# One two-bank PSUM tile for attention, then two one-bank tiles for layer 1 and Sinkhorn, with a new hand-written start order

## The chip, the core and the metric

The kernel runs on one core of one Trainium2 chip. The metric is device time in microseconds (us), the median of several executions. The profile is that of one further execution of the same program.

## What is computed

Linear attention over 8 batches, 8 heads, 576 positions and 64 channels feeds a mixture of 8 experts on 4608 tokens of width 512. The routing weights come from 8 Sinkhorn rounds over a 4608 x 8 matrix.

```python
phi = lambda x: np.where(x > 0, x, np.exp(x) - 1.0) + 1.0
q_p, k_p = phi(q), phi(k)
kv  = einsum('bhsd,bhse->bhde', k_p, v);   z = k_p.sum(axis=2)
x   = einsum('bhsd,bhde->bhse', q_p, kv) / (einsum('bhsd,bhd->bhs', q_p, z) + 1e-6)   # as [4608, 512]
logits = x @ w_gate;  P = exp(logits - logits.max())
for _ in range(8):
    P /= P.sum(1, keepdims=True) + 1e-9
    P /= P.sum(0, keepdims=True) + 1e-9
    P *= N / E
out = sum over e of  P[:, e:e+1] * (np.maximum(x @ w1[e], 0) @ w2[e])
```

## The kernel before

The kernel is a list of tasks for a small planner (`_Plan`). Each task has an engine (TensorE "pe", ScalarE "act", VectorE "dve", GpSimd's DMA issue "pool", SyncE's "sp", the transfer itself "dma", or "none" for bookkeeping), a planned duration, its predecessors and the buffers that it takes. The planner emits the tasks in the order of its planned start times. Each engine then executes its own instructions strictly in that order. The first 1465 tasks do not follow the planner's choice: their order is written out by hand in `_FRONT` (number of the task, letter of the engine). All waits between engines are put in by the tile framework: an instruction waits for the earlier instructions that wrote or read the same tile.

The stages are these.

- **Warm-up.** TensorE runs 46 dummy matmuls of 512 columns (line 575). They fill the time until attention's first inputs are there, and stand between attention's first steps after that.
- **Attention.** There are 16 groups (batch b, half g of the heads), n = 2b + g. A group loads k, q and v through one queue of GpSimd (line 366; the very first k goes through SyncE). ScalarE takes the exponentials of k and q (lines 376 and 435), VectorE builds phi (lines 380, 384, 438, 442). TensorE multiplies k and v ("KV", line 401), transposes q ("QT", line 427), multiplies for the denominator twice ("DEN", `f_den`, line 458) and for the numerator twice ("NUM", `f_num`, line 458). ScalarE inverts the denominator by Ln and Exp (lines 471, 476), and VectorE writes x, transposed, to `xT` (line 486). QT and DEN write the tile `at2`, 128 x 2 x 512 float32, two PSUM banks. KV and NUM share the other two-bank tile `kv_ps`.
- **Expert 0 as filler.** TensorE fills the gaps with layer 1 (line 659) and layer 2 (line 887) of expert 0 for the blocks of 512 tokens that attention has finished. The weights w1 of expert 0 come in four pieces and w2 in two, in the same GpSimd queue as q, k and v.
- **Logits and Sinkhorn.** Four small products (line 502) write a part of one bank of `at2`. When all are there, eight rounds run on VectorE (lines 526 to 536, 545 to 550), and in each a matmul with a matrix of ones sums over the partitions (line 541, `f_c`). It writes 8 columns of one bank of `at2`.
- **Experts 1 to 7.** From token block 5 of expert 0 on, layer 1 and layer 2 run as seven products of half size each (a Strassen-like scheme). `block7` is layer 1: two pairs per block, each with seven products of four matmuls (line 781), `m1` to `m7`. A pair holds three PSUM banks: `gX` (tile `hq`), `gZ` (tile `Zye`) and `gR`, which is one bank of `at2`, given out in turn by `att_bank()`. Into `gR` go `m5` (opens the bank) and `m3` (adds to it). Between them ScalarE copies it out (`f_s5`, line 807), and after them VectorE reads it once more (`f_h12`, line 816). Layer 2 is line 1005; VectorE adds its results to `acc` (line 1019), and builds the sums `S` (line 978), `W` (line 945) and `T` (line 957).

The order of the products from expert 1 on is a fixed chain on TensorE (lines 1089 to 1102).

PSUM has eight banks: two for `ye`, two for `hq`, two for `at2` and two for attention's `kv_ps`; the last two become `Zye` when attention is over (`f_close`).

```python
at2 = aps.tile([P, 2, 512], FP32, tag="att", name="att")           # line 256
def att_bank():                                                    # line 345
    return at2[:, (len(p_att["order"]) - 1) % 2]
```

Of the kernel before, what the change touches and what calls it, by code (L numbers as in the profile page):

```python
# [10 lines left out]
FP32 = mybir.dt.float32  # L11
# [6 lines left out]
class _Plan:  # L18
# [121 lines left out]
    1n 108n 119n 599n 109g 110m 48s 49m 2p 3p 50g 51m 4p 0g 5p 6p 52g 53m 7p 8p 76g 77m 9p 78g 79m 10p 11p 80g 81m  # L140
    12p 13p 14p 15p 126g 127m 16p 54a 55d 17p 18p 128g 129m 19p 20p 21p 22p 130g 131m 23p 24p 25p 26p 27p 61n 111g
    112m 62a 63d 28p 29p 56d 30p 31p 32p 33p 64d 34p 35p 36p 37p 57n 156g 157m 58p 65p 59a 82a 114g 115m 38p 66d 39p
    40p 83d 60a 89n 116g 117m 67p 84d 41p 68a 42p 91d 90a 69p 85n 154g 155m 43p 86p 70a 92d 158g 159m 71a 87d 93p
    133d 88a 94d 139n 182g 183m 132a 74p 95p 75d 44p 45p 96a 46p 134d 184g 185m 72p 140a 97p 73d 135n 47p 141d 98a
    136p 113n 186g 187m 142d 99a 137d 143p 138d 120g 121m 167n 600p 168a 144d 100p 101d 145p 601p 123g 124m 146a 169d
    102p 602p 103d 147p 603p 170d 148a 118n 210g 211m 604p 606p 149a 605d 608p 610p 161d 212g 213m 160a 152p 171p
    153d 612p 172a 162d 214g 215m 607d 163n 613a 164p 609d 611a 240g 241m 614p 165a 166d 189d 173p 195n 188a 242g
    243m 616p 615a 197d 190d 174a 150p 618p 268g 269m 196a 151d 191n 175p 636n 192p 176a 198d 177a 619d 199p 193d
    104g 105m 122n 622p 200d 194a 617a 180p 201p 181d 620p 202a 178p 203p 125n 179d 244g 245m 621p 204a 623p 628d
    106g 107m 217d 637p 639p 223n 216a 218d 270g 271m 224a 624p 225d 205a 226d 219n 272g 273m 220p 640d 638a 227p  # L150
    221a 298g 299m 641p 222a 228d 630a 208p 229p 253n 246a 302g 303m 209d 626p 230a 247d 643p 254a 642d 354g 355m
    231p 248d 206p 300g 301m 645p 232a 255d 207d 233a 625p 249n 256d 236p 644a 238p 237d 274a 281n 275d 250p 239a
    646a 257p 251d 330g 331m 647p 252d 258a 326g 327m 276d 649p 328g 329m 283d 282a 305d 259p 234p 627p 648a 235d
    277n 260a 651p 284d 650d 285p 669n 278p 286d 311n 304a 634a 261p 279d 358g 359m 670p 262a 280d 356g 357m 313d
    264p 263a 652d 287p 655p 671d 288a 265d 656p 312a 306d 266p 672p 267d 339n 307n 340a 289p 314d 308p 663a 290a
    659p 309d 386g 387m 332a 310d 384g 385m 315p 673d 292p 291a 382g 383m 316d 674p 341d 317p 632a 333d 660p 414g
    415m 318a 293d 676p 675a 342d 657p 361d 677a 360a 367n 334d 294p 319p 658p 295d 335n 320a 412g 413m 362d 336p
    321a 369d 343p 337d 416g 417m 678p 338a 344d 395n 440g 441m 665a 368a 324p 389d 345p 653p 325d 346a 679d 654p
    388a 322p 680p 323d 363n 396a 347p 397d 370d 364p 348a 661d 371p 446a 500g 501m 681d 682p 442g 443m 419d 365a
    686p 366a 372d 349a 352p 398d 296p 683a 390d 684p 297a 353d 667a 373p 685d 702n 350p 505g 374a 703p 496g 497m  # L160
    554n 560n 391n 351d 418a 425n 399p 392p 400d 468g 469m 375p 393d 444g 445m 688p 376a 394d 470g 471m 704d 689p
    377a 420d 401p 427d 378p 402a 687p 379d 696a 403p 447d 426a 380p 705p 381d 421n 404a 707p 448d 498g 499m 706d
    555g 556m 453n 474a 422p 428d 557g 558m 405a 692p 472g 473m 423a 429p 424a 709p 454a 430d 481n 408p 455d 710a
    431p 409d 693p 708a 578d 432a 406p 711p 407d 449n 694a 433p 456d 450p 434a 712d 435a 475d 457p 713p 476d 510n
    482a 483d 715p 458d 559n 451a 690p 452a 484d 714a 436p 700a 459p 437d 717p 460a 716d 438p 718a 461p 439d 477n
    691p 462a 512d 463a 503d 478p 735n 579d 485p 502a 479d 721p 486d 480a 736p 585d 504d 487p 722p 488a 580d 581s
    582m 466p 489p 467d 738p 490a 737d 511a 464p 410p 465d 506n 739a 698d 507p 411a 513d 740p 508a 729a 509a 514p
    741d 491a 742p 515d 492p 586d 516p 493d 719p 517a 564d 494p 518p 720p 565d 519a 566d 743d 725p 567s 568m 727a
    587d 520a 495d 726p 588s 589m 569s 570m 523p 723p 524d 583s 584m 744p 521p 746p 522d 724p 552n 747a 768d 745a
    772d 525p 733a 773d 748p 769d 774d 750p 731d 775s 776m 590s 591m 749d 754p 751a 779n 770d 526a 553p 527d 777s  # L170
    778m 755p 752p 780p 592d 528p 753p 781a 771d 794p 529d 782p 824d 786p 783a 762d 784p 787a 593d 788p 825d 796p
    571d 790p 797a 758p 760d 785a 791d 756p 795a 826d 530d 827s 828m 759p 792p 800p 757p 801a 766a 789d 798p 831n
    793a 804p 799a 531p 832p 805d 802p 833a 532d 806p 803d 838p 807a 764d 836p 839a 810p 594d 876d 595s 596m 834p
    597s 598m 533d 846p 835a 812p 837a 813p 847a 848p 877d 840p 849a 878d 842p 572d 854p 841d 852p 843d 811p 853a
    820a 855d 844p 818a 534p 850p 573d 845a 535d 814p 574s 575m 851a 536d 829s 830m 815p 856p 985s 986m 884p 576s
    577m 808p 885a 977d 809p 822d 857d 537p 886p 883n 538d 890p 887a 539d 866p 816a 891a 892p 888p 858p 889a 867p
    859a 893d 894p 874d 540p 898p 895d 864p 899a 541d 542d 896p 862p 897a 900p 902p 901a 863p 903a 928d 904p 929d
    865p 1042s 1043m 561g 562m 905a 930d 879s 880m 870a 881s 882m 906p 872d 543p 908p 544d 936p 909d 931s 932m 860p
    933s 934m 907d 861p 545d 938p 868a 935n 918p 937a 939a 919p 978d 910p 926a 546p 979d 942p 940p 547d 943a 944p
    911a 916p 945d 941a 563n 548d 946p 917p 950p 924a 952p 951a 914p 953a 947d 956p 980d 915p 957a 960p 954p 961d  # L180
    549p 948p 550d 962p 949a 551d 912p 922d 635a 958p 913p 631a 959d 1498n 1499g 1500m 963a 988p 1501g 1502m 920d
    987n 955a 970p 761d 989a 990p 976n 981d 763a 968p 982d 991a 994p 871d 996p 983d 995a 992p 697a 998p 971p 993a
    999d 699a 629d 969p 997d 1000p 975d 974a 1002p 1004p 1003a 964p 1005a 1503n 1008p 1010p 1009a 1006p 701a 1011d
    965p 1001a 984d 1012p 1007a 1045p 1013d 966p 1046a 633d 967p 1047p 973d 1044n 1504n 1014p 1048a 972d 1051p 1099s
    1100m 1015a 1053p 666a 1049p 1016d 1020p 1052a 1017d 1022p 1018d 1021a 662a 1019d 1025p 1050a 1023d 1055p 1024d
    664a 1030p 1056d 668d 1033p 1031d 1032d 1057p 1059p 1058a 1061p 1060a 1036p 1062a 1026a 1065p 1038d 1067p 1027g
    1037d 1066a 1063p 1054d 730a 1069p 1102p 1064a 1070d 1104p 1103a 1035d 1039p 1105a 1068d 1071p 1034d 1101n 1108p
    1040d 1072a 1156s 1157m 1041d 1110p 1109a 1073d 1106p 1028a 1077p 1074d 1029g 732d 1079p 1078a 1075d 734a 1082p
    1076d 1107a 1080d 1112p 1085a 1081d 1087p 873a 1113d 1086g 817a 869d 1090p 1089d 1083a 1088d 1114p 1084g 1111d
    1116p 1118p 728d 1117a 1093p 695d 1119a 927d 1115a 1092d 1122p 1091d 1124p 1123a 1095d 1120p 1094d 1126p 1121a  # L190
    1159p 1127d 1161p 1160a 1096p 1162a 1128p 1098d 1158n 1165p 1097d 1129a 1213s 1214m 1167p 1125d 1163p 1130d 1134p
    1131d 1136p 1135a 1132d 1166a 1139p 921d 1164a 1138d 1169p 1133d 1140a 1144p 1142a 1137d 1170d 1143g 1147p 1145d
    1141g 1146d 1171p 1148d 1173p 1172a 1508d 1175p 1174a 1150p 1509d 1176a 1168d 765a 1179p 1151d 1181p 1180a 1152d
    1177p 1183p 1178a 1216p 1184d 1218p 1217a 1149d 1153p 1219a 767d 1182d 1185p 1215n 1222p 1155d 1186a 1270s 1271m
    1154d 1224p 875a 823d 1220p 1187d 1191p 1223a 1188d 1193p 1192a 1189d 1196p 1190d 1195d 1226p 1199a 1194d 1201p
    1197a 1200g 1225d 1221a 1204p 1227d 1198g 1203d 1228p 1202d 1230p 1205d 1232p 1231a 1207p 1233a 1229a 1236p 1209d
    1238p 1206d 1237a 1234p 1239d 1240p 1235a 1273p 1208d 1275p 1241d 1274a 1210p 1276a 1242p 1212d 1272n 1279p 1211d
# [15 lines left out]
def kernel(  # L213
# [17 lines left out]
    P = 128  # L231
# [280 lines left out]
    def sinkhorn():  # L512
# [10 lines left out]
        for it in range(8):  # L523
# [15 lines left out]
            def f_c(_, gc=gc):  # L539
                gc["tile"] = att_bank()[:, 2 * E:3 * E]  # L540
                nc.tensor.matmul(gc["tile"], lhsT=ones_t, rhs=gs, start=True, stop=True)
# [65 lines left out]
    for b2, t in lg_pe.items():  # L607
        if 4 * b2 + 7 < len(kv_id):
            S_.dep(kv_id[4 * b2 + 7], t)
    p_done = sinkhorn()  # L610

    accp = []
    Zt = [None, None]

    def f_close(_):
# [521 lines left out]
```

## Time and profile before

| | |
|---|---|
| time, median of 3 runs | 970.51 us (969.93 to 971.1) |
| the profiled execution: its own time | 968.34 us |
| its span, first to last instruction | 966.5 us |
| granted TensorE clock over the span | 1.00 |
| TensorE matmul busy | 954.4 us (99% of the span), 8480 matmuls |
| VectorE busy | 774.7 us (80%) |
| ScalarE busy | 571.8 us (59%) |
| GpSimd busy | 145.8 us (15%) |

A row of the page's groups gives line, engine, operation, output<-inputs and shape, then the busy time of the group and the mean of one, then the idle time of the engine just before such instructions and what ended it. In a timeline, a row has its start, its length (merged rows are a run of equal instructions) and in brackets the idle time before it with the instruction that ended it. A matmul's row is longer than the distance between two matmuls, since the next one starts while the last one drains. So the idle time in brackets is less than what TensorE lost there.

### The profile page before, as it was taken

How to read it: one execution, taken by the hardware profiler on the slowest of the kernel's cores; microseconds unless marked ns; L12 is line 12 of the kernel's file. 1: busy time of each engine (PE TensorE's matmuls, PEld its weight loads, DVE VectorE, ACT ScalarE, POOL GpSimd, SP SyncE). 2: the span in 40 equal slices, each digit the busy share in tenths (PEclk: the TensorE clock that was granted, in tenths of full speed). 3: DMA queues.
4: the chain of work that ended last, by engine and by line, in shares of the span. 5: the costliest groups of instructions: out<-in, count | busy, mean ns of one | idle time of the engine just before them, and what ended most of it. 6: DMA issues, size and time to landing. Idle time of an engine off the chain costs nothing.

```text
span 966.5 us, 20909 instructions
## 1 busy us (share of the span) xinstructions
PE 954.4 (99%) x8480; PEld 795.6 (82%) x8480; DVE 774.7 (80%) x1484; ACT 571.8 (59%) x1017; POOL 145.8 (15%) x209
## 2 busy tenths in 40 slices
PE   8999999999999999999999999999999999999998
PEld 4565566688888888888888888888888888888886
DVE  5898898788878888878887888878887888877775
ACT  5898744665555555555555555555555555555553
POOL 6434000011022111111112111111112111111110
PEclk9999999999999999999999999999999999999999
DMA  9998646222257222262226322272225322235554
GB/s 224 260 203 187 158 143 207 45 77 78 77 120 163 79 77 78 86 156 77 78 76 123 113 70 73 74 159 71 76 77 132 107 77 77 78 99 164 164 164 109
DMA packets 45680, 112.50 MB, mean 116 GB/s; under 512 B 4368, under 2 KB 25616, under 8 KB 45584
## 3 DMA queue, kind: packets, MB, share of 16 engines
q1 hardware_dynamic: 21056, 75.57, 23.9%
q0 software_dynamic: 24128, 35.07, 19.3%
q8 instruction: 66, 1.08, 0.4%
q10 hardware_dynamic: 400, 0.52, 0.2%
q14 instruction: 30, 0.25, 0.1%
HBM read 119.69 MB, written 17.69 MB: 142 GB/s over the span
## 4 chain that ended last, share of the span: by engine, by line
PE 92%; DVE 3%; ACT 2%; issue 1%; DMA 1%; POOL 0%; DVEq 0%; POOLq 0%; ACTq 0%
PE ye L1005 32%; PE hq L781 23%; PE att L781 12%; PE ye L887 6%; PE Zye L781 6%; PE Zye L1005 5%; PE hq L659 3%; PE yw L575 1%; DVE h L816 1%; DVE acc L1019 1%; PE kv_ps L401 1%; PE att L458 1%; DVE S L978 1%; DMA kin<-in_k_dram 1%; PE num_ps L458 1%
## 5 line engine op out<-in xcount | busy, mean ns | idle before, releaser
L1019 DVE SCALAR_TENSOR_TENSOR acc<-ye,P_sb,acc 128x256 f32<-128x256 f32 x620 | 267.8, 479 | 123.9 <-PE ye L1005 122.9
L781 PEld LDWEIGHTS <-W 128*128 128x128 f16 x2144 | 209.8, 98 | 30.8 <-issue 2.5
L1005 PEld LDWEIGHTS <-S 128*128 128x128 f16 x1984 | 194.0, 98 | 23.4 <-DVE S L978 0.7
L1005 PE MATMUL ye<-T,S 128*128 128x256 f16 x1488 | 192.8, 273 | 0.4 <-DVE S L978 0.4
L1029 POOL TENSOR_TENSOR acc<-acc,st 128x256 f32<-128x256 f32 x124 | 88.1, 729 | 635.7 <-ACT st L1026 635.6
L781 PEld LDWEIGHTS <-w 128*128 128x128 f16 x1608 | 157.3, 98 | 21.2 <-issue 1.0
L813 ACT ACTIVATE h<-hq 128x512 f16<-128x512 f32 x134 | 80.0, 597 | 141.8 <-PE hq L781 140.6
L1005 PEld LDWEIGHTS <-h 128*128 128x128 f16 x1488 | 145.5, 98 | 17.6 <-issue 0.7
L781 PE MATMUL att<-xs,W 128*128 128x256 f16 x1008 | 151.2, 273 | 1.3 <-DVE h L816 1.2
L781 PE MATMUL hq<-xs,W 128*128 128x256 f16 x1008 | 151.2, 273 | 0.0
L781 PE MATMUL hq<-xs,w 128*128 128x256 f16 x1008 | 140.9, 273 | 0.3 <-DVE h L816 0.3
L810 ACT ACTIVATE h<-Zye 128x512 f16<-128x512 f32 x134 | 80.0, 597 | 38.3 <-PE Zye L781 38.3
L816 DVE CUSTOM_DVE_ANT_0 h<-att,s 128x512 f16<-128x512 f32 x126 | 86.5, 687 | 15.1 <-ACT s L800 13.0
L1026 ACT ACTIVATE st<-Zye,P_sb 128x256 f32<-128x256 f32 x124 | 52.7, 471 | 73.3 <-PE Zye L1005 73.3
L793 ACT COPY Zye<-hq 128x512 f32<-128x512 f32 x134 | 77.7, 580 | 28.9 <-PE hq L781 28.6
L978 DVE TENSOR_TENSOR S<-h 128x1024 f16<-128x1024 f16 x124 | 85.8, 692 | 11.0 <-ACT h L813 10.7
L800 ACT COPY s<-hq 128x512 f32<-128x512 f32 x126 | 73.5, 583 | 34.9 <-PE hq L781 34.8
L816 DVE CUSTOM_DVE_ANT_0 h<-hq,s 128x512 f16<-128x512 f32 x126 | 86.6, 687 | 4.0 <-PE hq L781 3.9
L887 PE MATMUL ye<-w,h 128*128 128x512 f16 x312 | 76.7, 379 | 0.0
L807 ACT COPY s<-att 128x512 f32<-128x512 f32 x126 | 74.6, 592 | 2.7 <-PE att L781 2.0
L781 PE MATMUL Zye<-xs,w 128*128 128x256 f16 x504 | 75.6, 273 | 0.0
L1005 PE MATMUL ye<-T,h 128*128 128x256 f16 x496 | 64.3, 273 | 0.3 <-DVE acc L1019 0.3
(104 smaller groups left out, 957.4 us busy)
## 6 DMA issues: line engine op xcount, KB each, us to landing
xs<-xd SPq DMA_DIRECT2D x63, 896.0 KB, 4.6
kin<-in_k_dram POOLq DMA_DIRECT2D x15, 576.0 KB, 6.9
out_dram<-acc SPq DMA_DIRECT2D x67, 128.0 KB, 2.4
w<-in_moe_w_dram POOLq DMA_DIRECT2D x16, 512.0 KB, 8.6
w<-in_moe_w_dram POOLq DMA_DIRECT2D x7, 1024.0 KB, 13.2
qin<-in_q_dram POOLq DMA_DIRECT2D x16, 288.0 KB, 6.2
vv<-in_v_dram POOLq DMA_DIRECT2D x16, 288.0 KB, 7.8
xd<-acc SPq DMA_DIRECT2D x5, 512.0 KB, 2.7
```

The source lines that it names most:

```text
L781: nc.tensor.matmul(dst[:, p, :], lhsT=lhs(p, c), rhs=rhs(c), start=(first and p == 0 and c == 0), stop=(c == 1), skip_group_check=True)
L793: nc.scalar.copy(out=Zt[1], in_=gX["tile"])
L800: nc.scalar.copy(out=gs2["tile"], in_=gX["tile"])
L807: nc.scalar.copy(out=gs5["tile"], in_=gR["tile"])
L810: nc.scalar.activation(out=hd(0, 0), in_=Zt[1], func=AF.Relu)
L813: nc.scalar.activation(out=hd(1, 0), in_=gX["tile"], func=AF.Relu)
L816: nc.vector._custom_dve(TENSOR_ADD_SAT, out=dst, in0=ps, in1=sb, s0=3.0e38, s1=0.0)
L887: nc.tensor.matmul(gy[tt]["tile"], lhsT=gh["tile"][:, f, ds(P * tt, P)], rhs=gw2["tile"][:, f, :], start=(f == 0), stop=(f == NFT - 1))
L978: nc.vector.tensor_tensor(out=Sx[:, i], in0=a0, in1=a1, op=op)
L1005: nc.tensor.matmul(bank(g_)[:, s, :], lhsT=lhs(s, kk), rhs=rhs(kk), start=(new and s == 0 and kk == 0), stop=(kk == 3), skip_group_check=True)
L1019: nc.vector.scalar_tensor_tensor(out=dst(), in0=bank(g_)[:, s, :], scalar=P_sb[:, gg, e:e + 1], in1=dst(), op0=ALU.mult, op1=ALU.add)
L1029: nc.gpsimd.tensor_tensor(out=dst(), in0=dst(), in1=gst["tile"], op=ALU.add)
```

## The change

There are three parts.

- **The tile.** The pool of `at2` gets a scope of its own (`aps_x`) and is placed at the other end of PSUM (`side="right"`). A new bookkeeping task `t_apsx`, after all of attention and all logits, closes it and opens in its place a pool with two tiles of one bank each, R0 and R1. `r_bank()` gives them out in the same turns as `att_bank()` did. Layer 1's `gR` and Sinkhorn's column sums use these; QT, DEN and the logits stay on `at2`. The first product into `gR` and the column sums get `t_apsx` as a further predecessor.
- **The planner's costs.** The transfer of a w1 piece goes from 1.6 to 1.4, the other weights from 2.75 to 2.6, and the latency of q, k and v from 2.3 to 2.2. These numbers only order the tasks behind the hand-written list.
- **The hand-written order.** `_FRONT` is replaced as a whole. Numbers from 527 on move by one, as `t_apsx` takes number 527. Task for task TensorE, GpSimd and SyncE have the same work in both lists, in another order. Of the tasks that may run on ScalarE or VectorE, some change sides; three of attention's copies of QT's result (`f_qc`, line 448) go from VectorE to ScalarE.

```diff
 _FRONT = """
-    1n 108n 119n 599n 109g 110m 48s 49m 2p 3p 50g 51m 4p 0g 5p 6p 52g 53m 7p 8p 76g 77m 9p 78g 79m 10p 11p 80g 81m
-    12p 13p 14p 15p 126g 127m 16p 54a 55d 17p 18p 128g 129m 19p 20p 21p 22p 130g 131m 23p 24p 25p 26p 27p 61n 111g
...
+    1n 104g 105m 108n 119n 600n 48s 49m 2p 3p 50g 51m 4p 76g 77m 5p 6p 52g 53m 7p 8p 78g 79m 9p 10p 126g 127m 54a 55d
+    11p 12p 80g 81m 13p 14p 15p 128g 129m 16p 56d 17p 18p 19p 130g 131m 20p 21p 22p 0g 23p 24p 25p 109g 110m 26p 27p
+    28p 82a 83d 29p 111g 112m 30p 31p 32p 33p 84d 34p 35p 36p 37p 38p 57n 58p 89n 61n 62a 63d 64d 156g 157m 65p 59a
...
 """
-    aps = ctx.enter_context(tc.tile_pool(name="aps", bufs=1, space=PSUM))
+    aps_x = ExitStack()
+    aps = aps_x.enter_context(tc.tile_pool(name="aps", bufs=1, space=PSUM, side="right"))
...
-                ts_.append(add(("dma", (1.6 if nm == "w1" and len(pieces) > 1 else 2.75)), lambda _: None, deps=[ti],
+                ts_.append(add(("dma", (1.4 if nm == "w1" and len(pieces) > 1 else 2.6)), lambda _: None, deps=[ti],
...
-            tin[nm] = fadd(("dma", 1.47 if nm == "k" else 1.42 if n else 2.3), lambda _: None, deps=[ti], use=[gr, *gsw], prio=pr, lat=2.3)
+            tin[nm] = fadd(("dma", 1.47 if nm == "k" else 1.42 if n else 2.3), lambda _: None, deps=[ti], use=[gr, *gsw], prio=pr, lat=2.2)
...
             def f_c(_, gc=gc):
-                gc["tile"] = att_bank()[:, 2 * E:3 * E]
+                gc["tile"] = r_bank()[:, 0, 2 * E:3 * E]
                 nc.tensor.matmul(gc["tile"], lhsT=ones_t, rhs=gs, start=True, stop=True)
...
-            c = add(("pe", 0.112), f_c, deps=[a], acq=[gc], prio=-200.0, lat=0.1)
+            c = add(("pe", 0.112), f_c, deps=[a, t_apsx], acq=[gc], prio=-200.0, lat=0.1)
...
+    Rt = []
+
+    def f_apsx(_):
+        aps_x.close()
+        rps = ctx.enter_context(tc.tile_pool(name="rps", bufs=1, space=PSUM, side="right"))
+        Rt.extend(rps.tile([P, 2, 256], FP32, tag=f"att{i}", name=f"R{i}") for i in range(2))
+
+    def r_bank():
+        return Rt[(len(p_att["order"]) - 1) % 2]
+    t_apsx = add(("none", 0.0), f_apsx, deps=[*front_ids, *lg_done], prio=0.0)
     p_done = sinkhorn()
...
                         g_["tile"] = (hqp.tile([P, 2, 256], FP32, tag="hq", name="hq") if g_ is gX else
-                                      att_bank().rearrange("p (a b) -> p a b", a=2))
+                                      r_bank())
...
-            m5 = pm(W(1, gi), T(1), gR, True, [m1, tW], 0.05)
+            m5 = pm(W(1, gi), T(1), gR, True, [m1, tW, t_apsx], 0.05)
```

In the list, 104 and 106 are the two tiny loads of the gate's weights, 109, 111, 114 and 116 the four pieces of expert 0's w1, 0 the identity matrix for QT; 48 to 53 are group 0's k, q and v, 76 to 81 group 1's, 126 to 131 group 2's. 54 and 82 are the exponentials of k of groups 0 and 1, 62 that of q of group 0; 2 to 47 are the dummy matmuls, 58 is KV and 65 QT of group 0.

## The prediction

> **What bounds the kernel now.** I read the page first.
>
> ```profile
> PE 954.4 (99%) x8480; PEld 795.6 (82%) x8480; DVE 774.7 (80%) x1484; ACT 571.8 (59%) x1017; POOL 145.8 (15%) x209
> PE   8999999999999999999999999999999999999998
> PEclk9999999999999999999999999999999999999999
> PE 92%; DVE 3%; ACT 2%; issue 1%; DMA 1%; POOL 0%; DVEq 0%; POOLq 0%; ACTq 0%
> ```
>
> TensorE is busy in 99% of the span at full granted clock, and holds 92% of the chain that ended last. Only the time in which it does no useful matmul can be won. The windows show where that is (columns: length, then busy us of each engine).
>
> ```profile
> 0.00:20.00 20.00, 16.43 (x105) 7.84 (x106) 9.86 (x19) 10.09 (x12) 13.87 (x25) 1.00 1.00 214
> 20.00:40.00 20.00, 18.77 (x156) 10.54 (x155) 17.68 (x29) 18.13 (x24) 8.85 (x12) 1.00 1.17 259
> 140.00:160.00 20.00, 19.58 (x132) 12.62 (x130) 18.04 (x44) 9.51 (x19) 0.00 (x0) 1.00 0.57 169
> 200.00:300.00 100.00, 97.97 (x885) 86.14 (x883) 82.77 (x162) 59.64 (x113) 13.97 (x19) 1.00 0.29 86
> 300.00:500.00 200.00, 200.00 (x1835) 179.26 (x1832) 160.42 (x309) 113.15 (x213) 27.14 (x38) 1.00 0.34 95
> 900.00:966.50 66.50, 62.30 (x546) 53.10 (x543) 45.33 (x88) 31.11 (x58) 6.55 (x10) 1.00 0.54 142
> ```
>
> Busy time flatters the start (dummy matmuls) and hides small waits (a matmul's row is longer than the distance to the next). So I made a ledger from the starts of all matmuls: each useful one counts its usual distance to the next (216 ns for 512 columns, 109 for 256 from line 781 on, 122 for line 458, 56 for QT, 45 for KV, 26 for logits), and the rest is lost. Lost by 24 us: 18.2; by 110: 22.4; by 140: 22.4; by 160: 23.5; by 200: 23.2; by 290: 27.0; by 945: 28.1; by 961: 28.7; after the last matmul 3.9 more. From 300 us on nothing is left to win but the tail, which keeps its instructions. What the change can touch: the start (18.2), attention (4.2, of which about 3.2 are the changes into and out of KV's half-height shape, 96 and 130 ns in each of 14 groups, and stay), 140 to 160 (1.1), 200 to 290 (3.8).
>
> Third, the group of products into the split tile, and a place in the timeline.
>
> ```profile
> L781 PE MATMUL att<-xs,W 128*128 128x256 f16 x1008 | 151.2, 273 | 1.3 <-DVE h L816 1.2
> ```
>
> ```profile
> 212.84 1.04 PE L781 MATMUL hq<-xs,w 128*128 128x256 f16 x8
> ...
> 213.62 0.67 DVE L816 CUSTOM_DVE_ANT_0 h<-att,s 128x512 f16<-128x512 f32 x1
> ...
> 214.34 0.60 PE L781 MATMUL att<-xs,W 128*128 128x256 f16 x4 [0.47 <-DVE h L816]
> ```
>
> Here m5 opens a bank of `at2` and waits until VectorE has read the pair before, which lies in the other bank. By the starts 0.63 us is lost. The waits written into the program of before confirm it: products into one half wait for readers of the other half. Following these waits through the trace gives seven stalls on VectorE's reading of the other bank: column sums at 148.17 us (0.17) and 157.82 (0.16), layer 1 at 214.34 (0.63), 229.29 (0.39), 255.82 (0.33), 283.74 (0.46) and 636.22 (0.09). Sum 2.24 us. Other waits into `att` in that time (131.45, 145.49, 266.55; 0.09, 0.40, 0.26) are on ScalarE's copy of the same bank and stay.
>
> **The two tiles.** They take away the seven waits. Upper end: all 2.24, plus every other wait of TensorE on VectorE or ScalarE from 140 to 290 us (2.5 more: 145.49, 147.57, 207.86, 211.97, 222.30, 266.55, 267.53, 281.54), if the new order loses none. Lower end: 0, if VectorE is late anyhow and TensorE meets it one product later. From 222 to 229 us VectorE was busy 6.84 of 7.00 us, so the 0.39 at 229.29 is its own lateness, and I count it as coming back. At the other six VectorE has slack nearby (5.75 of 8.00 us from 214 to 222, 13.19 of 17.00 from 267 to 284). I take 2.24 - 0.39 = 1.85 us won.
>
> The Trainium skill's page "PSUM — Partial Sum Buffer", section "PSUM bank collisions raise a hardware error", states that two engines collide by bank and quadrant, and run clean on different banks. By it alone all seven waits are needless and this term is 2.24, the time 0.39 us less than mine; the trace shows the waits, not what stands behind them.
>
> Closing and reopening issues no instruction. The first writers of R0 and R1 must wait for the old tile's last reader, the last logits' Exp, over at 126.0 us; the first column sum came at 128.5 and the first m5 at 130.1, so 2.5 us cover it. Without cover it would be the lateness of that Exp, for the column sum and the layer-1 products queued behind it. Another position in PSUM changes no row: 0. The planner's costs issue nothing.
>
> **The new order, start.** Landings are read from the trace's DMA records. In before, one w1 piece (256 KB) is ahead of q in GpSimd's queue; it landed at 6.88, then q0 8.42, v0 9.83, k1 11.29, q1 12.61, v1 14.12, k2 15.55, q2 16.88, v2 18.40, w1's second piece 19.66: one each 1.3 to 1.5 us. After, a 4 KB load (0.16 us by the pair at 45.72 and 45.88) goes first, both w1 pieces come behind v2, and k1 ahead of v0. q0 is issued at about 2.3. The shortest landing of such a load in the trace is 4.03 us, so it lands between 6.3 and 8.4; I take 7.0, one piece earlier. Then k1 8.5, v0 9.9, q1 11.3, k2 12.8, v1 14.2, q2 15.5, v2 17.0, the w1 pair 19.5. From group 4 on the same items have gone through, so the landings are the same.
>
> Now the three queues with before's durations (before's start in brackets). KV0 stands behind 37 dummies instead of 36, 0.21 each: 12.1 (11.89); QT0 12.95 (12.74). ScalarE does k1's Exp at 8.5 and q0's by 10.8, not at 13.18 between the two copies of KV0's result, so these end at 13.8 (14.73). DEN0 now waits for VectorE's copy of QT0: 14.5 (14.79). ScalarE then runs q1's Exp, Ln (14.95), k2's Exp, Ln to 17.45: KV1 16.0 (16.59), QT1 17.5 (17.88), NUM0 18.05 and 19.75 (19.30, 20.62), x of group 0 done 20.95 (21.90). KV2 21.0 (21.96), QT2 22.1 (23.19), NUM1 22.85 (24.14), DEN2 23.55 (24.79). Layer 1 starts at 23.8 (23.70), with NUM1 and DEN2 already behind it. QT3 26.65 (28.78), KV3 28.95 (30.54). In before four more layer-1 matmuls (4 x 0.216 = 0.87) come ahead of KV3: won 30.54 - 0.87 - 28.95 = 0.72 us. Ends: 1.5 if q1, k2 and the rest land early too; 0.9 lost if k1 lands at 11.29 as before, because q0's Exp is now queued behind k1's on ScalarE: Exp to 13.6, QT0 14.4, some 1.6 late.
>
> **The new order, attention.** The 14 shape changes stay. True waits after 24 us came to about 1 us. ScalarE gets three more copies (1.12 us each, VectorE's are 0.76): counted by rows, ScalarE's work up to the last Exp of attention rises from 94.4 to 96.4 us, VectorE's from 85.2 to 85.9. The trace shows no run of this order: between -0.8 and +5, by the rival below. I take 0, since the work per queue is the same within 2%.
>
> **Later order.** From the third product after the last column sum TensorE's sequence is nearly that of before and from expert 2 on the planner makes it by the same rule; 645 us there lost 1 us. 0.
>
> **Sum.** 0.72 + 1.85 = 2.57 us won. The profiled execution took 968.34 (span 966.5 and 1.8 around it), 2.17 below the runs' median of 970.51. So the next profile should show a span near 964.0 and its own time near 965.8, and the median 967.9 us. A difference under 0.2% (1.94 us) is about what can't be told from none.
>
> **Rivals.**
>
> - *Attention's queue is late* (slower). TensorE is in order and each of 16 groups puts seven products in its queue. In before about ten of these waited, 0.2 to 0.5 us each, 0.3 on average (for instance 30.54: 0.39, 58.82: 0.27, 80.94: 0.50). One more such wait per group costs 16 x 0.3 = 4.9 us, net 970.5 - 2.6 + 4.9 = 972.8. It decides from (1.94 + 2.57) / 16 = 0.28 us per group. For it: ScalarE was busy 18.1 to 18.5 of 20 us there and gets more; the whole list is new. Against: before's list, of the same kind, has few waits. 0.16.
> - *The wait moves* (same). VectorE is the late one from 200 to 290 us, the products wait one step later, or the two tiles still hold each other up, as they share a pool: only the start is won, 969.8. For it: 82.8% busy there with full stretches. Against: slack at six of seven places. 0.23.
> - *The start fails* (same): k1 late, 970.5 - 1.85 + 0.9 = 969.6. 0.07.
> - *More is won*: the new order has none of the other waits from 140 to 290 either: 970.5 - 0.7 - 2.2 - 2.0 = 965.6. 0.14.
> - *The forecast*, 967.2 to 968.6: 0.40.
>
> So faster by over 0.2%: 0.40 + 0.14 = 0.54; within 0.2%: 0.23 + 0.07 = 0.30; slower: 0.16. The range reaches from 965.0, just past the fourth rival, to 972.8, the middle of the first, which leaves half of 0.16 and a few hundredths out.
>
> **What would show it.** Right: the group `att` of line 781 without idle time on line 816; the windows 200 to 300 and 140 to 160 with TensorE nearer to full; KV3 near 29 us with four fewer layer-1 matmuls ahead. Wrong: q0 landing at 8.4 or k1 at 11.3; new idle rows at lines 401, 427 and 458 between 24 and 110 us, or a ledger there above 4.2; idle on VectorE's `acc` or `S` (lines 1019, 978) in place of line 816.

## The result and the profile after

The changed kernel takes 966.60 us (median of 6 runs, 965.53 to 968.68) against 970.23 us in the same comparison (6 runs, 969.56 to 971.42): ratio 0.9964, 95% interval 0.9950 to 0.9978. The forecast was 967.9. The profiled execution took 966.83 us, span 965.0. First its page:

```profile
PE 953.1 (99%) x8480; PEld 796.4 (83%) x8480; DVE 771.6 (80%) x1479; ACT 576.2 (60%) x1022; POOL 145.5 (15%) x209
PE   8999899999999999999999999999999999999998
PEclk9999999999999999999999999999999999999999
PE 93%; DMA 3%; DVE 2%; ACT 1%; issue 0%; POOL 0%; POOLq 0%; ACTq 0%; DVEq 0%
```

In the second row one slice, the fifth (97 to 121 us), has fallen to 8, and DMA has 3% of the chain instead of 1%. The windows (columns as before) say more:

```profile
110.00:120.00 10.00, 7.52 (x53) 3.98 (x51) 6.57 (x13) 6.04 (x8) 0.00 (x0) 0.83 0.79 187
140.00:160.00 20.00, 20.00 (x142) 13.68 (x140) 14.79 (x38) 11.50 (x22) 0.00 (x0) 1.00 0.64 206
200.00:300.00 100.00, 100.00 (x918) 89.57 (x916) 86.23 (x170) 59.92 (x113) 16.40 (x23) 1.00 0.37 100
```

From 140 to 160 and from 200 to 300 us TensorE is now busy without a gap (19.58 and 97.97 before). But from 110 to 120 us it is busy only 7.52 of 10 us, at a granted clock of 0.83: a stall that before did not have. The group of layer 1's products into the split tile has no idle time left (1.3 us before):

```profile
L792 PE MATMUL R<-xs,W 128*128 128x256 f16 x1008 | 151.2, 273 | 0.0
```

The ledger of the prediction, taken for every profile of this study, gives the us lost in four stretches. (A little below zero means that the usual distances were put a few ns too high; the small added matmuls of the last experiments count as lost time.)

| kernel | 0-24 | 24-110 | 110-130 | 130-300 | median us | ratio to before (interval) |
|---|---|---|---|---|---|---|
| before | 18.2 | 4.2 | 0.0 | 4.7 | 970.2 to 971.0 | |
| changed | 17.4 | 4.3 | 4.4 | -0.4 | 966.60 | 0.9964 (0.9950-0.9978) |
| changed, again | 17.4 | 3.9 | 3.9 | -0.4 | 965.96 | 0.9957 (0.9942-0.9973) |
| tiles only | 18.4 | 5.3 | 0.1 | 3.7 | 966.30 | 0.9953 (0.9936-0.9971) |
| order only | 17.7 | 5.9 | 2.8 | 5.1 | 971.86 | 1.0012 (1.0000-1.0024) |
| changed, loads early | 17.4 | 6.1 | 0.2 | -0.5 | 964.92 | 0.9941 (0.9928-0.9953) |
| the same, w1 piece first | 18.7 | 5.3 | 0.2 | -0.4 | 964.86 | 0.9934 (0.9922-0.9946) |
| order only, loads early | 17.4 | 5.4 | 0.2 | 5.2 | 969.21 | 0.9988 (0.9978-0.9998) |
| tiles only, w2 early | 17.9 | 5.0 | 0.2 | -0.3 | 964.97 | 0.9937 (0.9922-0.9952) |
| before, w2 early | 17.9 | 7.4 | 0.1 | 4.7 | 969.92 | 0.9985 (0.9971-1.0000) |

So the profiles show 0.8 us won at the start and 5.1 after 130 us, and 4.4 lost again in a place that the prediction did not have.

### The profile page after: what moved, and what is told of

It reads as the page before. It is cut to its first block, busy times and chain, and to the rows that moved or that the text cites. A ratio compares the mean times of both kernels' runs of the same rounds, so it can differ in the third digit from the quotient of the medians.

```text
span 965.0 us, 20849 instructions
## 1 busy us (share of the span) xinstructions
PE 953.1 (99%) x8480; PEld 796.4 (83%) x8480; DVE 771.6 (80%) x1479; ACT 576.2 (60%) x1022; POOL 145.5 (15%) x209
## 4 chain that ended last, share of the span: by engine, by line
PE 93%; DMA 3%; DVE 2%; ACT 1%; issue 0%; POOL 0%; POOLq 0%; ACTq 0%; DVEq 0%
PE ye L1016 33%; PE hq L792 24%; PE R L792 12%; PE ye L898 6%; PE Zye L792 6%; PE Zye L1016 6%; PE hq L670 2%; DMA kin<-in_k_dram 2%; DMA xd<-acc 1%; PE kv_ps L402 1%; PE att L459 1%; PE num_ps L459 0%; PE att L428 0%; ACT ek L377 0%; DVE qpT L329 0%
## 5 line engine op out<-in xcount | busy, mean ns | idle before, releaser
L792 PE MATMUL R<-xs,W 128*128 128x256 f16 x1008 | 151.2, 273 | 0.0
L827 DVE CUSTOM_DVE_ANT_0 h<-R,s 128x512 f16<-128x512 f32 x126 | 86.5, 687 | 12.4 <-ACT s L811 12.4
L818 ACT COPY s<-R 128x512 f32<-128x512 f32 x126 | 74.5, 591 | 0.7 <-PE R L792 0.7
L1016 PE MATMUL ye<-w,h 128*128 128x256 f16 x496 | 64.3, 273 | 0.0
```

Of the source, the lines that this page charges most:

```text
L792: nc.tensor.matmul(dst[:, p, :], lhsT=lhs(p, c), rhs=rhs(c), start=(first and p == 0 and c == 0), stop=(c == 1), skip_group_check=True)
L818: nc.scalar.copy(out=gs5["tile"], in_=gR["tile"])
L827: nc.vector._custom_dve(TENSOR_ADD_SAT, out=dst, in0=ps, in1=sb, s0=3.0e38, s1=0.0)
L1016: nc.tensor.matmul(bank(g_)[:, s, :], lhsT=lhs(s, kk), rhs=rhs(kk), start=(new and s == 0 and kk == 0), stop=(kk == 3), skip_group_check=True)
```

## The experiments

**Is the stall there every time?** The changed kernel once more.

> The changed kernel once more, to see whether its second profile shows the same stall. In the first, VectorE waits 2.86 us at 111.8 us for a store of xd that landed 9.96 us after its issue, behind expert 1's three weight loads, and TensorE loses about 4.3 us by 120 us (2.65 us of waiting, the rest at a lower granted clock). Theory: the stall is in every execution, since GpSimd issues these loads at 99.7 to 101.9 us and the store follows at 101.8; expected are a store that lands 7 to 11 us after its issue, a loss of 4.0 to 4.6 us between 110 and 120 us, and 3.6 us less than before (ratio 0.995 to 0.998). Rival: it was an accident of one execution; then the second profile has no such stall and its own time is near 962.5 us.

Measured: 965.96 us (965.08 to 968.43), and the same stall in the second profile: the store landed 9.39 us after its issue, VectorE waited 2.3 us, 3.9 us were lost. It belongs to the order. In the timeline of the changed kernel's first profile it looks like this:

```profile
95.31 0.71 POOL L367 DMA_DIRECT2D vv<-in_v_dram  x1 [7.80 <-PE kv_ps L402]
99.48 0.19 POOL L393 CAST gate<-vv 128x4 f32<-128x4 f16 x1 [3.46 <-DMA vv<-in_v_dram]
99.72 1.54 POOL L302 DMA_DIRECT2D w<-in_moe_w_dram  x2
101.85 0.62 POOL L302 DMA_DIRECT2D w<-in_moe_w_dram  x1 [0.58 <-issue]
101.83 17.08 SPq L726 DMA_DIRECT2D xd<-acc  x3
111.81 0.42 DVE L710 TENSOR_TENSOR acc<-xT 128x512 f16<-128x512 f16 x1 [2.86 <-DMA xd<-acc]
113.16 0.68 DVE L677 TENSOR_SCALAR h<-hq 128x512 f16<-128x512 f32 x1
113.89 1.86 PE L670 MATMUL hq<-xT,w 128*128 128x512 f16 x4 [2.48 <-DVE h L677]
```

Read from the bottom: layer 1 waits for VectorE's `h`; VectorE is in order and stands in front of `x_blocks` (line 710), which wants its staging buffer back; the buffer is held by a store of 512 KB, issued at 101.83 and landed at 111.79. The same kind of store takes 2.65 us when nothing is ahead of it. (SP's row merges three stores; this is the first.) Ahead of it are expert 1's three loads, 2 MB, issued from 99.72 on, right behind a small cast that waits for the last v. In before's timeline two of these loads stand ahead of the last v that is issued and one behind it. They had all landed by 107.82, and the store came only at 108.29:

```profile
91.59 1.27 POOL L301 DMA_DIRECT2D w<-in_moe_w_dram  x2
92.81 0.75 POOL L366 DMA_DIRECT2D vv<-in_v_dram  x1
94.44 1.18 POOL L301 DMA_DIRECT2D w<-in_moe_w_dram  x1 [0.88 <-issue]
```

**Tiles alone.** Before's list with every number from 527 on moved by one, "527n" after "526a", and before's costs.

> Before's hand-written order and planner's costs, and only the two one-bank tiles. Theory: the seven waits on the other bank go and nothing else, 1.85 to 2.24 us less than before (ratio 0.9977 to 0.9981), no idle time on line 827 in the group of products into att, and the other waits of 140 to 290 us (ScalarE's copy, acc, S; 2.4 us) still there. Rival 1: the tiles alone bring everything that the changed kernel won from 140 to 290 us, 5.0 us less (ratio 0.995). Rival 2: the products wait one step later and nothing is won (ratio 1.000).

Measured: 966.30 us (964.45 to 968.63). Rival 1 holds: by 280 us the tiles alone have removed everything but 0.09 us at 132.77, TensorE's own waits on the other bank and also those on ScalarE's copy, `acc` and `S`. Two groups of VectorE from 126 to 300 us, before and then with the tiles alone, show what the prediction left out:

```profile
L816 DVE CUSTOM_DVE_ANT_0 h<-att,s 128x512 f16<-128x512 f32 x19 | 13.0, 685 | 5.3 <-ACT s L800 3.7 <-PE att L781 1.0 <-ACT s L807 0.4
L816 DVE CUSTOM_DVE_ANT_0 h<-att,acc 128x512 f16<-128x512 f32 x8 | 5.4, 680 | 1.5 <-PE att L781 1.4
```

```profile
L826 DVE CUSTOM_DVE_ANT_0 h<-R,s 128x512 f16<-128x512 f32 x19 | 13.0, 682 | 3.3 <-ACT s L810 3.3
L826 DVE CUSTOM_DVE_ANT_0 h<-R,acc 128x512 f16<-128x512 f32 x8 | 5.5, 686 | 1.1 <-PE R L791 0.7 <-ACT acc L810 0.3
```

The readers of the tile waited on each other too. In the profile before, none of VectorE's 134 reads by `f_h12` runs beside ScalarE's copy `f_s5` out of the other bank; with the tiles alone four do. One of these places in the two timelines, before and tiles alone:

```profile
205.31 0.59 ACT L807 COPY s<-att 128x512 f32<-128x512 f32 x1
205.94 0.69 DVE L816 CUSTOM_DVE_ANT_0 h<-att,s 128x512 f16<-128x512 f32 x1 [0.41 <-ACT s L807]
```

```profile
205.36 0.59 ACT L817 COPY s<-R 128x512 f32<-128x512 f32 x1
205.49 0.68 DVE L826 CUSTOM_DVE_ANT_0 h<-R,s 128x512 f16<-128x512 f32 x1
```

Before, VectorE starts when ScalarE's copy is over; with two tiles it reads its bank beside it, 0.45 us earlier.

The readers also waited for TensorE's products into the other bank. The idle time on `PE att` in the first pair of groups above is of this kind in three places: at 146.22 us (0.68), 220.76 (0.54) and 279.62 (0.49). Before:

```profile
144.21 0.60 PE L781 MATMUL att<-xT,W 128*128 128x256 f16 x4
145.49 0.60 PE L781 MATMUL att<-xT,W 128*128 128x256 f16 x4 [0.24 <-ACT acc L807]
146.22 0.69 DVE L816 CUSTOM_DVE_ANT_0 h<-att,acc 128x512 f16<-128x512 f32 x1 [0.68 <-PE att L781]
```

The products of 144.21 complete the bank that `h` reads; it starts only when those of 145.49, into the other bank, are over. The same place in the kernel "tiles only, w2 early" of the table:

```profile
144.84 0.60 PE L791 MATMUL R<-xT,W 128*128 128x256 f16 x4
145.72 0.60 PE L791 MATMUL R<-xT,W 128*128 128x256 f16 x4
145.82 0.68 DVE L826 CUSTOM_DVE_ANT_0 h<-R,acc 128x512 f16<-128x512 f32 x1
```

In the four profiles of a two-bank tile, none of 276 reads of VectorE and ScalarE from 128 us on runs beside a product into the other bank. In the six of the changed kernel, the tiles alone and their versions with moved loads, 11 to 19 do. TensorE loses its 0.54 us at 222.30 on `S` and its 0.48 at 281.54 on `acc` right behind the late reads of 220.76 and 279.62.

The profiled execution was the slowest of the five, with a new wait at the end of the stretch:

```profile
281.17 0.69 DVE L967 TENSOR_TENSOR T<-w 128x1024 f16<-128x1024 f16 x1 [2.32 <-DMA w<-in_moe_w_dram]
283.30 1.69 PE L1015 MATMUL ye<-w,h 128*128 128x256 f16 x8 [2.10 <-DVE acc L1029]
```

Expert 2's w2 was issued at 268.89 behind GpSimd's additions, as in before, and landed 12.26 us later; TensorE had come some 4 us nearer to it.

**Order alone.** The changed kernel, where the two halves stay one tile.

```diff
-        aps_x.close()
-        rps = ctx.enter_context(tc.tile_pool(name="rps", ...))
-        Rt.extend(rps.tile([P, 2, 256], FP32, tag=f"att{i}", name=f"R{i}") for i in range(2))
+        Rt.extend(at2[:, i].rearrange("p (a b) -> p a b", a=2) for i in range(2))
```

> The changed kernel's hand-written order and costs with attention's two-bank tile kept to the end (the two names R0 and R1 are its halves). Theory: the waits on the other bank come back, 1.85 to 2.24 us over the changed kernel (968.5 to 968.8, ratio to before 0.9982 to 0.9987), with the stall of 4.3 us before 120 us unchanged. Rival 1: the new order alone has no waits from 140 to 290 us, because TensorE's stall at 113 us lets VectorE and ScalarE get ahead; then it equals the changed kernel (ratio 0.996). Rival 2: the tiles are the cause of all 5.0 us won from 140 to 290; then it is at 971.6 (ratio 1.0014).

Measured: 971.86 us, near rival 2's 971.6: the tiles are the cause of the whole gain after 130 us (5.1 us lost there without them, -0.4 with them). The new order by itself gains nothing; it is even with before or up to 0.24% slower.

**The loads early.** The list's "562g", "556g" and "558g" (with their transfers) go ahead of "500g", the last v, and lose the dependence on the cast:

```diff
-    w_t[1] = load_w1(1, prio=0.0, deps=[gates[15]]) + load_w2(1, prio=0.0, deps=[gates[15]])
+    w_t[1] = load_w1(1, prio=0.0) + load_w2(1, prio=0.0)
```

> The changed kernel with expert 1's three weight loads (2 MB) put ahead of the last load of v in GpSimd's queue (and not held back by the small cast that waits for v), so issued from 87.5 us on instead of 99.7. Theory: they are through the DMA engines by about 105 us, the store issued at 101.8 lands before 108.9 us, when VectorE comes to its buffer, and the stall of 4.3 us goes: 962.3 us (ratio to before 0.992). Rival 1: part of what was won from 140 to 290 us was won because TensorE's stall let VectorE catch up; then up to 2.8 us come back as waits there, 965.1 (ratio 0.9947). Rival 2: the last v or q lands late behind the loads and attention waits in its place: 966 to 968 (ratio 0.996 to 0.998).

Measured: 964.92 us (964.30 to 965.43). The loads were issued from 88.34 us on and had landed by 106.44; the store of 103.52 landed at 109.39, and VectorE passes without a wait:

```profile
110.55 0.41 DVE L709 TENSOR_TENSOR acc<-xT 128x512 f16<-128x512 f16 x1
```

The stall is gone (0.2 us), and nothing came back after 130 us, so rival 1 falls: the gain there is not a gift of the stall. Rival 2 falls too: the last v landed at 108.86 instead of 99.43, but no product waited for it. The median fell by 1.0 us against the changed kernel in the same comparison, by 1.7 against the first, not by 4.3. The profile shows 1.8 us more lost from 24 to 110 us, in waits ahead of anything that was moved (27.46: 1.29, 85.99: 0.96). A second part is on record in the granted clock. In 5 of 11 executions of the changed kernel it was 0.998 over the span, as in both profiles, where it fell to half for 3.41 us behind the stall; these five took 965.95 to 968.68 us. The other six, at 1.00, took 965.08 to 966.83, and all five of this kernel were at 0.999 or 1.00. So both profiles may show a dearer form of the stall than the median execution had; where the clock fell in the executions without a profile is not known, and whether this is the whole of the difference is open.

**Tiles with before's order and w2 early.** "1506g 1507m" go from behind "1315g" to behind "1199g".

> The two tiles with before's hand-written order, and one load moved in GpSimd's queue: expert 2's w2 (1 MB) is issued after the eighth addition of GpSimd's partial results (about 239 us) instead of the twelfth (268.9 us in the profile of the tiles alone). There VectorE waited 2.32 us at 281.2 for this load, TensorE lost 3.9 us with the lower clock behind it, and the five times reached from 964.5 to 968.6. Theory: before's list left this load about 10 us, as much as it takes to land, and TensorE's gain used up the margin; with the load 30 us earlier no execution waits, the waits of 140 to 300 us are gone altogether, and the median is 964.3 to 964.9 with a spread under 2 us (ratio to before 0.9933 to 0.9938). Rival: the wait was an accident of one execution, the spread has other causes, and the median stays at 966.3 (ratio 0.9953).

Measured: 964.97 us (963.11 to 966.98), as the theory had it, with a spread of 3.9 us that it had not; the profile loses nothing from 130 to 300 us. Before's order with two tiles and one load moved is as fast as the changed kernel with its loads moved, so the new list was not needed for the gain.

**Order alone with the loads early.**

> The new order with the two-bank tile kept and with expert 1's loads early: the new order by itself, without the stall at 113 us. Theory 1: order alone is worth the start's 0.7 us or less, so about 969.5 to 970.5 (ratio to before 0.9985 to 1.0), and the waits on the other bank cost 5 us against the version with tiles (964.9). Theory 2 (the order is adapted to the two tiles, and bad without them): like the order alone with the stall, 971 to 972 less 1.8, near 970.1, with 1 to 2 us more lost from 200 to 300 us than before's 3.8. Rival: without the stall before it the waits grow, 972.

Measured: 969.21 us, 0.9988 (0.9978 to 0.9998). The windows from 200 to 300 us, this kernel and then the one with tiles, before's order and w2 early:

```profile
200.00:300.00 100.00, 97.50 (x881) 85.65 (x879) 82.87 (x162) 58.46 (x109) 15.00 (x21) 1.00 0.34 92
```

```profile
200.00:300.00 100.00, 100.00 (x919) 89.60 (x917) 84.45 (x166) 61.76 (x117) 16.39 (x22) 1.00 0.34 95
```

The tiles are worth 4.3 us by these medians (969.21 - 964.92), the loads' place 2.65 (971.86 - 969.21). Each pair was timed in different comparisons; by the ratios to before it is 4.6 and 2.3.

**The start undone.** In the version with early loads, "109g 110m" go back ahead of "48s".

> The version with early loads, and the first w1 piece (two loads of 128 KB) put ahead of q and k in GpSimd's queue, as in before. It undoes the start's step alone. Theory (the prediction's): q0 lands at 8.3 to 8.5 us instead of 7.4, k1 and the others one place later too, KV0 and QT0 stay behind the dummy matmuls, and DEN0 and KV1 come 0.5 to 1 us later; 0.7 us more than with q first (964.9): 965.6. Rival 1: the start's gain is given back by 30 us in any case, since from group 3 on the queue is as full as before, then 964.9. Rival 2: ScalarE's Exp of q0, queued behind k1's, makes QT0 late by 1 us and the whole costs 1.5 to 2: 966.5 to 967.

Measured: 964.86 us, the same as with q first: rival 1. The profile has the theory's step (q0 lands at 9.25 instead of 7.48, KV1 starts at 17.41 instead of 15.37, 1.3 us more are lost by 24 us), and by 110 us less than half a microsecond is left. At 85.99 us the version with q first waits 0.96 us on ScalarE, which itself had waited 0.9 us for a load of k; that wait is gone when TensorE comes later. In this pair of profiles most of what is won at the start is waited for there. The two profiles of the changed kernel have no such wait, so that it is always so is not shown; the equal medians are.

**Which waits were it?** Four kernels on "tiles only, w2 early" bring single kinds of wait back, up to expert 1. A small matmul of 8 columns ahead of `m5`, into its own tile (control) or into the other one (then TensorE waits for the other bank's reader again), and a small read of the other tile by ScalarE ahead of `f_s5` (then ScalarE waits for the other bank's users again, and VectorE for ScalarE's small read):

```diff
+ nc.tensor.matmul(Rt[1 - i][:, 0, 0:8], lhsT=lhs(0, 0), rhs=rhs(0)[:, 0:8], start=True, stop=True, ...)   # control: Rt[i]
+ nc.scalar.copy(out=scr, in_=Rt[1 - gR["i"]][:, 0, 16:24])
```

> Control. The tiles with before's order and the early w2 load (964.97 us), and 15 small matmuls of 8 columns on TensorE, each ahead of a pair's m5 (up to expert 1) and into m5's own bank, where m5 starts anew. They add no wait that m5 does not have. Both theories: 15 times 0.05 to 0.13 us more, 965.7 to 967, the loss spread over 130 to 300 us.

> The same 15 small matmuls, but into the other tile, whose 8 columns nobody reads any more. So TensorE again waits, before m5, until the other tile's last reader on VectorE is done, as it did with the two-bank tile; VectorE and ScalarE have no wait of before's on the other bank. Theory of the prediction (what was won is TensorE's own seven waits, 2.24 us, of which layer 1's five are 1.9): 1.9 us more than the control. Rival (most of what was won is that VectorE and ScalarE no longer wait for each other across the banks, and TensorE's waits were late because these were): less than 0.8 us more than the control.

> The tiles with before's order and the early w2 load, and ahead of ScalarE's copy of a pair's first product (up to expert 1, 26 times) a small copy of 8 columns of the other tile into a scratch tile, which nobody reads. It brings back the waits between the two readers: VectorE's h12 waits for ScalarE's small copy in 9 places, as in the program of before, and ScalarE's for VectorE's column-sum or h12 reads in 14. TensorE has next to no new wait. Theory of the prediction: 0 to 0.3 us more (964.97 to 965.3). Rival: 1.5 to 3 us more (966.5 to 968), lost from 140 to 300 us on acc, S and ScalarE's copy.

> Both: the small matmuls into the other tile and ScalarE's small reads of it. It stands for the two-bank tile with before's order and the early w2 load. Expected of both theories: what before lost from 140 to 290 us (4.6) comes back beside the control's cost, 970 to 971; if it stays 1.5 us or more below the control plus 4, the two kinds of wait are not the whole of what the tiles removed.

| | median us | median at a granted clock of 0.999 or more (executions) | lost 130 to 300 us |
|---|---|---|---|
| base | 964.97 | 964.00 (3 of 6) | -0.3 |
| control | 964.51 | 963.45 (3 of 6) | 0.1 |
| TensorE's waits | 965.93 | 965.36 (4 of 6) | 1.0 |
| readers' waits | 966.59 | 965.36 (3 of 6) | 0.8 |
| both | 965.90 | 965.80 (5 of 6) | 2.2 |
| before, w2 early | 969.92 | 969.56 (6 of 12) | 4.7 |

The medians of all executions are too close for this, and two miss their forecasts: the control is below the base, and both together 4 us below 970. Some executions lost time to a lower clock. The few at full clock come in the ledger's order: 1.9 us for TensorE's waits and 2.4 for both against the control, 1.4 for the readers' against the base, 5.6 for before. What each wait cost is read from the profiles. Against the control TensorE's waits cost 0.9 us, and they come back at two of the predicted places with before's sizes (0.60 and 0.33; the two were 0.63 and 0.33). The timeline of that kernel shows the larger one, with the small matmul as the one that waits:

```profile
212.43 0.17 PE L798 MATMUL R<-xs,W 128*128 128x8 f16 x1 [0.44 <-DVE h L838]
212.46 0.60 PE L803 MATMUL R<-xs,W 128*128 128x256 f16 x4
```

The readers' waits cost 1.1 us against the base, and TensorE loses them where the prediction had said "stay": 0.47 and 0.33 on ScalarE's copy (0.40 and 0.26 before), 0.13 on `S`. Ahead of the 0.47 the small read waited for TensorE's products into the other tile, ahead of the 0.33 for VectorE's read of it, each as ScalarE's copy did before (144.85, 265.91). Together they cost 2.1 against the control, the sum of the two. So neither theory was the whole: own waits and readers' waits are of like size.

Of the 5.0 us between the base and before with w2 early, 2.9 were not brought back. The column sums, which were left alone, are 0.33 of it. The added instructions also stand for less than the whole tile. The small read takes 0.17 us where the copy takes 0.59: at 208.52 us of the readers' kernel VectorE again reads beside ScalarE's copy, where it waited 0.41 before. And VectorE still does not wait for TensorE's products into the other tile: 9 to 12 of its reads run beside them in these kernels, none in before. That wait, 0.5 to 0.7 us in three places before, is the likely rest; no run brings it back alone, so its share is not shown.

**The control for that.** Before with its w2 early:

> The kernel before (two-bank tile, its own order) with expert 2's w2 load moved forward in GpSimd's queue, as in the version with tiles and the early load. It is the two-bank kernel against which that version (964.97 us), and the one with both kinds of wait brought back (2.1 us lost from 130 to 300 us), are to be held. Theory: the load alone changes nothing while the waits on the other bank hold TensorE back, 970.2 to 970.9 (ratio 0.999 to 1.001) with 4.2 to 4.8 us lost from 130 to 300; then the small matmuls and reads brought back somewhat under half of the tiles' effect. Rival: the load's place in the queue was behind the waits at 281.5 and 283.7 us (0.94 us) and more, 968.5 to 969.5, with 2 to 3.7 us lost there; then the two kinds of wait are most of what the tiles removed, and part of the rest was the load.

Measured: 969.92 us, and the ledger from 130 to 300 us has before's waits one by one (0.40, 0.34, 0.16, 0.16, 0.63, 0.54, 0.39, 0.33, 0.26, 0.48, 0.46 among them), 4.7 in all. The load is not behind them.

## Why the prediction was near, and where it was not

- **The seven waits** were real and of the stated size where they could be brought back singly. The mis-sized term is the tiles' worth: 1.85 us taken, 2.24 the mechanism's upper end, 5.1 measured in the profile (4.6 to 5.3 by the ratios to before of kernels with and without tiles). The step that failed is the sentence that the waits of 145.49 and 266.55 "are on ScalarE's copy of the same bank and stay"; those on `acc` and `S` were left to the new order. TensorE's wait was on the same bank, but ScalarE and VectorE had themselves waited on the other one, for each other and for TensorE's products. The prediction searched the waits of TensorE for the other bank, not those of the readers. It also gave back 0.39 at 229.29, since VectorE was busy 6.84 of 7.00 us; that wait is gone as well. A busy VectorE was no proof that it was the bound.
- The Trainium skill's page "PSUM — Partial Sum Buffer", section "PSUM bank collisions raise a hardware error", which the prediction weighed for TensorE alone, counts a ScalarE read beside a VectorE read of one bank too, and lets different banks run side by side. The timelines at 205 us agree: with two tiles the two reads overlap from 205.49 to 205.95, with one tile they do not.
- **"More is won"** (0.14) is what the stretch from 130 us on did. It was named as the new order's doing; the runs show that it is the tiles'.
- **The start** came as worked out: q0 landed at 7.54 (7.0), k1 9.01 (8.5); QT0 12.27 (12.95), KV1 15.37 (16.0), KV2 20.14 (21.0), QT3 26.57 (26.65), KV3 28.89 (28.95), four layer-1 products fewer ahead of it. KV0 was 1.1 early because five fewer of the first dummies ran at half speed (7 instead of 12; 6 to 13 in all profiles), which is chance. By 24 us five profiles of the new start have lost 17.4 or 17.7 us, eight of before's start (those with added matmuls and reads among them) 17.5 to 18.7, 18.1 on average: some 0.6 won. That it lasts to the end was the unchecked step: with the start undone the time is the same.
- **Attention's order** at 0 holds: 24 to 110 us lost 3.9 to 6.1 us in five profiles of the new order with q first, 4.2 to 7.4 in four of before's list (before, tiles only, and both with w2 early). The longest waits there stand at the same places in most profiles; their length, 0.5 to 2.8 us, differs between executions (last section). (The prediction's "true waits of about 1 us" does not fit the ten waits of 0.3 us that it gives under its first rival.)
- **The stall** at 113 us was not among the rivals. The working followed GpSimd's queue only as far as the start; it did not follow the three loads of expert 1, which the list moves past the last v, to the SP store behind them. That is 2.8 to 4.4 us in the three profiles that have it, 1.0 to 2.7 by the medians.
- **Later order** at 0 was wrong by a load: expert 2's w2 is issued at 238.8 us instead of 271.5, which took away the margin problem that the tiles alone run into. (The two orders of TensorE agree from about thirty products after the last column sum on, not from the third.)
- **The offset.** Before's profile was 2.2 us below its median, the changed one 0.2 above. The profiles differ by 1.5 us and the medians by 3.6, so an own time of 965.8 was forecast and 966.83 came, while the median came 1.3 lower than forecast. The gain that was forecast too small and the loss that was not forecast cancelled most of each other: that the time came so near is luck.

## What to carry to other kernels

When two banks share one tile, list the waits of all who touch it, readers on each other and on products into the other bank included, and expect more from splitting it than the writer's own waits. When an order is replaced, follow each large load to what is issued behind it on any queue, and to the buffer that this holds. A gain in TensorE's own path brings it nearer to loads whose issue hangs on something else; check their margin.

## What was not expected of the hardware

- **A short stall costs more than its length.** Six gaps of 2.1 to 2.8 us in TensorE's work were seen after the start; behind five of them the granted clock was 0.50 for 3.41 us, which cost some 1.3 to 1.7 us more (the four matmuls at 113.89 above took 1.86 us instead of 1.03). Behind one, 2.60 us in the order-only kernel, almost nothing was slow, and behind the eight gaps of 0.9 to 1.7 us likewise. The Trainium skill's page "TensorE: Matmul & The Clock Gate", Part 1, puts the half clock behind an idle window of about 3.4 us; the half rate agrees (granted clock 0.50 from 114 to 116 us), but here shorter gaps were enough.
- **A store takes longer beside loads of another queue.** SP's 512 KB store took 9.96 us beside GpSimd's 2 MB, 5.88 with the loads early, when one of the three was in, the others landed 0.4 and 2.9 us later and the last v 5.3, and 2.65 alone.
- **Landings are uneven, mostly at the same loads.** With GpSimd's queue full, most loads of q, k and v land 1.3 to 1.6 us behind the one before, but some 2 to 4.6. With before's list the v of group 12 is 2.4 to 4.4 us behind in all eight profiles, and `num_ps` waits 0.5 to 2.8 us at 80.5 to 83.2 us in all eight. With the new list the k of group 3 is 2.5 to 3.3 us behind in five of six profiles (24.71 behind 21.74 in the changed kernel); in four of the five with q first QT3 then waits 0.6 to 1.3 us at 27 us. So the place goes with the order of the loads and the size with the execution. What makes these loads late was not tried, nor how much of the spread of single times follows from it.
